# First query tile of chunk 0 finished first and copied out in fp32, last query tile in its bank, key banks and VectorE's order changed

## The chip, the cores and the metric

The kernel runs on one core of a Trainium2 chip. Its engines work in parallel, each through its own queue in order: TensorE (PE in the profile; its weight loads are PEld), VectorE (DVE), ScalarE (ACT), GpSimd (POOL), and SyncE (SP), whose queue issues the DMAs. They wait for each other through semaphores. The metric is the device time of one execution in microseconds; three runs of the kernel before gave 827.88, 828.29 and 828.38 us, a median of 828.29.

## The reference

One transformer layer over 2048 tokens of width 1024, in bf16. A conditioning vector `c` gives six rows of scales and shifts. A layer norm, scaled and shifted, feeds a linear attention of 32 heads; a second one feeds a gated feed-forward of width 3584; both are added back to `x`. What matters here is the front of the attention:

```python
mod = (_silu(c) @ w_mod).reshape(c.shape[0], 6, 1, -1)
sa, ca, ga, sb, cb, gb = (mod[:, 0].copy(), ..., mod[:, 5].copy())
h = _layernorm(x, axis=-1) * (1 + ca) + sa
...
phi = lambda t: jnp.where(t > 0, t + 1, jnp.exp(t)) + 1e-06
pq, pk = (phi(q), phi(k))          # q, k, v are the three thirds of h @ wqkv
kv = jnp.einsum('bhsd,bhse->bhde', pk, v)
z = jnp.einsum('bhsd->bhd', pk)
num = jnp.einsum('bhqd,bhde->bhqe', pq, kv)
den = jnp.einsum('bhqd,bhd->bhq', pq, z)[..., None] + 1e-06
```

## The kernel before

The program is recorded as one list of operations; each is put on its engine's queue in the order in which it is written. `auto` (line 168) records an operation, `add` (line 130) finds whom it must wait for: overlapping bytes in SBUF, and in PSUM whole banks (`self.excl`, line 156): an operation waits for the last access of every other engine to the same 2 KB bank. There is no scheduler: the written order is the order on each queue, and all operations carry the line of the recording helper, L176.

The 2048 tokens are handled in four chunks of 512, each of four x tiles of 128 tokens. The normalised tile is transposed by a DMA on SP's queue (`th_dma`, line 493) into `HT`, which has two buffers, and there scaled and shifted (`th_mod`, line 497; `MODCOL` holds the columns). For a chunk, a group of 8 products (128 weight columns by 512 tokens) gives one eighth of the queries (`q_group`, line 708) or keys (`k_group`, line 715) in one PSUM bank; `next_bank` (line 703) hands out the banks.

The function `phi` is made from a bank by `phi_evac` (line 665) and `phi_flush` (line 677). ScalarE writes an exponential to a slot of `E1` (four slots, in turn), and for queries also a relu to `RL`. When two groups have been through ScalarE, VectorE does the pair: a minimum with 1 on each slot, then for keys a pass that reads the bank once more and writes `PKT` (two buffers), for queries an addition into `PQT`. A key bank is thus free when VectorE has read it, a query bank when ScalarE has.

Chunk 0's queries are special (`q_phase_chunk0`, line 773), since the modulation columns are still being made from arriving weights. Seven of the eight query tiles, in banks 1, 2, 3, 4, 6, 7, 5, are accumulated in parts while the columns come (`q_part`, line 696). Bank 0 collects the columns of scale, shift and bias: `mod_sc` (line 508) makes shift columns out of `WSA`, `fin_sa` (line 519) copies them out, `bias_mm` (line 532) makes from them what the missing shift of the first four eighths of the inner dimension would have added to the queries, and `bias_fin` (line 538) copies it to `BIASQ`. The shift itself is put on these parts of `HT` afterwards (`h0_shift`, line 528), for the keys. The eighth query tile is computed in bank 0 after `bias_fin`. Then ScalarE makes exponential and relu of all eight tiles with `BIASQ` as bias (`q_phi`, line 759), into `E1` and `RL` for tiles 0 to 3, `E1X` and `RLX` for tiles 4 to 7; `q_min` and `q_add` (lines 763 and 768) are VectorE's part.

Around it stands the layer norm of chunk 1's x tiles 4 to 7: tile 4's sums by ScalarE (`act_stats`, line 578), the others' by VectorE (`ln_ops`), then a power on GpSimd (`ln1_rstd1`, `ln1_rstd2`, `pool_pow`), a normalising pass on VectorE and the transpose. Tile 5 goes first, then 4, 6 and 7.

After that come the eight key groups of chunk 0, with side work taken from `kside` (line 852) behind groups 1, 3 and 4: `th_mod` of chunk 1, each eighth in two halves of 256 tokens, the last query pair (6, 7), and ScalarE's sums for x tiles 10 and 11. Chunk 1 then begins with its own key groups (`chunk`, line 870), which read the whole 512 tokens of each eighth of `HT`.

Of the kernel before, what the change touches and what calls it, by code (L numbers as in the profile page):

```python
# [262 lines left out]
def bass_adaLN_cond__linear_attn_block__swiglu_ffn__prompt_kernel(  # L263
# [22 lines left out]
    with ExitStack() as es:  # L286
# [6 lines left out]
        def T(name, off, shape, dt):  # L293
            n = 1
            for s_ in shape[1:]:
                n *= s_
            assert off % 32 == 0 and off + n * mybir.dt.size(dt) <= ARENA, (name, off, shape)
            return nc.alloc_sbuf_tensor_at(name, shape, dt, offset=base + off)
# [49 lines left out]
        RLX = T("rlx", 196 * KB, [128, 4, 512], BF16)  # L348
        ACC = T("acc", 192 * KB, [128, D], FP32)
# [178 lines left out]
        def h0_shift(dt):  # L528
            P.dve("tensor_scalar", out=HT[:, 0, dt, :], in0=HT[:, 0, dt, :], scalar1=MODCOL[:, 1, dt:dt + 1],
                  scalar2=None, op0=ALU.add)  # L530
# [172 lines left out]
        def next_bank():  # L703
            i = qk_ctr[0]
            qk_ctr[0] += 1
            return (1, 2, 3, 4, 6, 7, 5, 0)[i % 8] if i < 40 else i % 5 + 1
# [48 lines left out]

        def q_slot(nt):
            return (E1, RL) if nt < 4 else (E1X, RLX)

        def q_phi(nt, bank):
            for buf, fn_ in zip(q_slot(nt), (ACT.Exp, ACT.Relu)):  # L760
                P.act("activation", out=buf[:, nt % 4, :], in_=PS[:, bank, :], func=fn_, bias=BIASQ[:, nt:nt + 1])

        def q_min(nts):
            for nt in nts:
                e = q_slot(nt)[0][:, nt % 4, :]
                P.dve("tensor_scalar", out=e, in0=e, scalar1=1.0, scalar2=1e-6, op0=ALU.min, op1=ALU.add)

        def q_add(nts):
            for nt in nts:
                e, r = q_slot(nt)  # L770
                P.dve("tensor_tensor", out=PQT[:, nt, 0:512], in0=r[:, nt % 4, :], in1=e[:, nt % 4, :], op=ALU.add)

        def q_phase_chunk0():
# [14 lines left out]
            act_stats(4, (0,))  # L788
# [15 lines left out]
            for nt in range(7):  # L804
                if nt == 1:
                    mod_sc(WSA, 0, range(4), range(4))
                if nt == 3:
                    mod_sc(WSA, 0, range(4), range(4, 8))
                    fin_sa(0, 4, True)
                    ln_ops[1][0]()  # L810
                if nt == 5:
                    bias_mm(range(4))
                    bias_fin()
                q_part(nt, qb[nt], (7,))
# [3 lines left out]
            for i, dt in enumerate((4, 5, 0, 1, 2, 3, 6, 7)):  # L818
                P.pe("matmul", out=PS[:, 0, :], lhsT=WQK[:, dt, 896:1024], rhs=HT[:, 0, dt, :], start=(i == 0),
                     stop=(i == 7))  # L820
            for dt in range(4):
                h0_shift(dt)
            ln1_xn(5)
            th_dma(5)
            for nt in range(2):
                q_phi(nt, qb[nt])
            act_stats(4, (1,))
            for nt in range(2, 8):
                q_phi(nt, qb[nt] if nt < 7 else 0)
# [9 lines left out]
            q_min((0, 1))  # L839
# [3 lines left out]
            q_add((0, 1))  # L843
            for nts in ((2, 3), (4, 5)):
                q_min(nts)
                q_add(nts)
# [8 lines left out]
        for c0 in (0, 256):  # L855
            for dt in range(NDT):
                add(kside, 1, lambda dt=dt, c0=c0: th_mod(1, dt, c0, c0 + 256))
        add(kside, 1, lambda: q_min((6, 7)))
        add(kside, 1, lambda: q_add((6, 7)))
        for jj, k in ((0, 3), (1, 4)):  # L860
            add(kside, k, lambda jj=jj: act_stats(10 + jj))
# [386 lines left out]
```

## Time and profile before

| what | us |
| --- | --- |
| median of the three runs | 828.29 |
| the profiled execution's own time | 827.71 |
| its span | 826.0 |
| TensorE busy with products | 816.3 |
| VectorE busy | 312.2 |
| ScalarE busy | 197.0 |
| GpSimd busy | 41.0 |

The granted clock of TensorE is 1.00. The span is the time from the first to the last instruction of the profiled execution; the execution's own time has a little around it. The views in order of time list, for one engine, start, length, the operation with the tile that it writes and those that it reads, and in brackets how long the engine had been idle and who ended that. Neighbours of one kind are merged into one row, whose length goes from the first start to the last end. The stage of the change lies between 24 and 60 us: chunk 0's queries end near 29 us, its keys near 43 us, and chunk 1's keys follow.

### The profile page before, as it was taken

To read this page: it belongs to the slowest core of one execution; us is meant where nothing else is said; L and a number is where in the kernel's file an instruction comes from. 1 tells how busy PE (TensorE), PEld (TensorE's weight loads), DVE (VectorE), ACT (ScalarE), POOL (GpSimd) and SP (SyncE) were. 2 spreads that over 40 slices of the span, in tenths; PEclk is the share of its full clock that TensorE was granted. 3 is DMA by queue.
4 is the path that set the end of the run, shared out by engine and by line. 5 is a ranking of instruction groups with operands and counts; after the bars stand their busy time and mean duration, and the time that the engine had idled before them with its cause. 6 is when DMAs were issued, how large, how long until landed. Compare 5 with 4: busy or idle time off the path is not lost.

```text
span 826.0 us, 10436 instructions
## 1 busy us (share of the span) xinstructions
PE 816.3 (99%) x4243; PEld 375.9 (46%) x4322; DVE 312.2 (38%) x672; ACT 197.0 (24%) x338; POOL 41.0 (5%) x58
## 2 busy tenths in 40 slices
PE   8999999999999999999999999999999999999998
PEld 4544444444444444444444444444444444444444
DVE  5798988477945521111221112122111111221111
ACT  4758642123341111011111101111110111111011
POOL 1110000000130000020000003000000300000000
DMA  9969756865698995600455570045557004553000
GB/s 316 297 139 223 167 159 149 181 175 211 149 253 245 296 249 153 166 26 26 136 151 151 153 174 25 23 131 153 151 152 182 27 19 126 151 152 88 0 26 26
DMA packets 199392, 119.32 MB, mean 144 GB/s; under 512 B 58024, under 2 KB 183088, under 8 KB 199344
## 3 DMA queue, kind: packets, MB, share of 16 engines
q1 hardware_dynamic: 199328, 118.65, 53.8%
q8 instruction: 34, 0.56, 0.3%
q14 instruction: 14, 0.11, 0.0%
q10 hardware_dynamic: 16, 0.00, 0.0%
HBM read 100.67 MB, written 4.33 MB: 127 GB/s over the span
## 4 chain that ended last, share of the span: by engine, by line
PE 98%; issue 1%; DMA 0%; DVE 0%; POOL 0%; SPq 0%
PE ps L176 98%; DMA xres<-in_A_x_dram 0%; POOL rstd L176 0%; DVE xres L176 0%; DVE stats L176 0%; SPq L176 0%; DVE ht L176 0%; DVE ve L176 0%; DVE mv L176 0%; DVE modcol L176 0%
## 5 line engine op out<-in xcount | busy, mean ns | idle before, releaser
L176 PE MATMUL ps<-h2t,gug 128*128 128x512 bf16 x878 | 210.1, 379 | 0.9
L176 PE MATMUL ps<-h2t,guu 128*128 128x512 bf16 x878 | 209.9, 379 | 0.9
L176 DVE TENSOR_TENSOR at<-sg,ps 128x512 bf16<-128x512 bf16 x112 | 77.0, 687 | 282.8 <-PE ps L176 270.6
L176 ACT ACTIVATE sg<-ps 128x512 bf16<-128x512 f32 x112 | 66.9, 597 | 309.7 <-PE ps L176 298.3
L176 PEld LDWEIGHTS ps<-h2t,guu 128*128 128x128 bf16 x896 | 87.7, 98 | 105.7
L176 PEld LDWEIGHTS ps<-h2t,gug 128*128 128x128 bf16 x896 | 87.6, 98 | 105.5
L176 PE MATMUL ps<-wd_a,at 128*128 128x512 bf16 (+1 forms) x502 | 111.9, 377 | 0.5
L176 PE MATMUL ps<-ht,wqk 128*128 128x512 bf16 x499 | 110.7, 379 | 0.9 <-DVE ht L176 0.2
L176 PE MATMUL ps<-wd_b,at 128*128 128x512 bf16 (+1 forms) x377 | 84.6, 377 | 0.4
L176 PEld LDWEIGHTS ps<-wd_a,at 128*128 128x128 bf16 x512 | 50.1, 98 | 59.6
L176 DVE TENSOR_TENSOR ut<-att,gb_b 128x512 bf16<-128x512 bf16 (+1 forms) x32 | 13.6, 426 | 167.5 <-ACT att L176 167.5
L176 PEld LDWEIGHTS ps<-ht,wqk 128*128 128x128 bf16 x512 | 49.2, 98 | 58.9 <-DVE ht L176 1.0
L176 ACT ACTIVATE att<-ps 128x512 bf16<-128x512 f32 (+1 forms) x32 | 17.4, 591 | 182.1 <-PE ps L176 182.1
L176 PEld LDWEIGHTS ps<-wd_b,at 128*128 128x128 bf16 x384 | 37.6, 98 | 44.7
L176 PE MATMUL ps<-pk,xres 128*128 128x512 bf16 x250 | 55.4, 379 | 0.6 <-issue 0.5
L176 PE MATMUL ps<-mw,pqt 128*128 128x512 bf16 x249 | 55.4, 379 | 0.5 <-issue 0.2
L176 POOL TENSOR_SCALAR h2t<-h2t,modcol 128x512 bf16<-128x512 bf16 x32 | 26.5, 846 | 383.0 <-DMA h2t<-xn 383.0
L176 ACT ACTIVATE e<-ps 128x512 bf16<-128x512 f32 x56 | 33.3, 611 | 31.8 <-PE ps L176 15.8
L176 ACT ACTIVATE junk<-xres 128x1024 bf16<-128x1024 bf16 x26 | 27.6, 1063 | 45.9 <-DVE xres L176 34.2
L176 PEld LDWEIGHTS ps<-mw,pqt 128*128 128x128 bf16 x256 | 24.8, 98 | 30.0 <-issue 0.5
L176 PEld LDWEIGHTS ps<-pk,xres 128*128 128x128 bf16 x256 | 24.6, 98 | 30.1 <-issue 1.3
L176 DVE SCALAR_TENSOR_TENSOR xres<-ps,xres 128x512 bf16<-128x512 f32 x32 | 21.5, 688 | 11.6 <-PE ps L176 11.3
(111 smaller groups left out, 337.8 us busy)
## 6 DMA issues: line engine op xcount, KB each, us to landing
gug<-in_B_w_gate_dram SPq DMA_DIRECT2D x56, 512.0 KB, 4.0
guu<-in_B_w_up_dram SPq DMA_DIRECT2D x56, 512.0 KB, 5.3
xres<-in_A_x_dram SPq DMA_DIRECT2D x20, 256.0 KB, 4.4
rb<-recip_den SPq DMA_DIRECT2D x8, 512.0 KB, 11.7
stgx<-in_w_mod_dram SPq DMA_DIRECT2D x2, 2048.0 KB, 9.3
wd_a<-in_B_w_down_dram SPq DMA_DIRECT2D x4, 1024.0 KB, 7.7
out_dram<-xres SPq DMA_DIRECT2D x31, 128.0 KB, 1.7
xres<-in_A_x_dram SPq DMA_DIRECT2D x3, 1024.0 KB, 6.5
```

Of the source, the lines that this page charges most:

```text
L176: return getattr(e, method)(**kw)
```

## The change

- Query tile 0 gets its last product first, and ScalarE copies its bank, without bias, to a new fp32 tile `QRAW`. Tile 0's exponential and relu are made from that copy, and come last of the eight (`QORD`). The four slots of `E1` and `RL` now hold tiles 1 to 4, those of `E1X` and `RLX` tiles 5, 6, 7 and 0.
- The eighth tile (tile 7) is computed in bank 1, which tile 0 has left. Its products stand around the last shift products, `fin_sa` and the bias products, in the order 0 to 7.
- Both passes of ScalarE's sums for x tile 4 come behind the copy; before, one stood earlier and one between the tiles' exponentials.
- On VectorE the four `h0_shift` come directly behind `bias_fin`, ahead of the rest of tile 5's statistics.
- The banks of chunk 0's key groups are 0, 2, 3, 4, 6, 7, 5, 1, and later groups up to the fortieth use 0, 2, 3, 1, 4, 6, 7, 5 in turn.
- Chunk 1's first halves of `th_mod` come ahead of the key groups, the second halves behind key group 1. The query pairs at positions 4 and 6 come behind key group 3. The sums of x tiles 10 and 11 come behind key groups 4 and 5 in place of 3 and 4.

```diff
@@ -346,6 +346,7 @@
         RL = T("rl", 188 * KB, [128, 4, 512], BF16)
         E1X = T("e1x", 192 * KB, [128, 4, 512], BF16)
         RLX = T("rlx", 196 * KB, [128, 4, 512], BF16)
+        QRAW = T("qraw", 202 * KB, [128, 512], FP32)
         ACC = T("acc", 192 * KB, [128, D], FP32)
         MHL = T("mhl", 196 * KB, [128, 2, D], BF16)
         MHLT = T("mhlt", 192 * KB, [128, 2 * NDT, 128], BF16)
@@ -703,7 +704,9 @@
         def next_bank():
             i = qk_ctr[0]
             qk_ctr[0] += 1
-            return (1, 2, 3, 4, 6, 7, 5, 0)[i % 8] if i < 40 else i % 5 + 1
+            if i < 8:
+                return (0, 2, 3, 4, 6, 7, 5, 1)[i]
+            return (0, 2, 3, 1, 4, 6, 7, 5)[i % 8] if i < 40 else i % 5 + 1
 
         def q_group(ch, nt):
             buf, bank = ch % 2, next_bank()
@@ -753,22 +756,30 @@
             P.wait_for("sp", [wr])
             P.dma("mdr%d" % i, dst[:], MDR[i].unsqueeze(0).to_broadcast([128, D]))
 
+        QORD = (1, 2, 3, 4, 5, 6, 7, 0)
+
         def q_slot(nt):
-            return (E1, RL) if nt < 4 else (E1X, RLX)
-
-        def q_phi(nt, bank):
+            i = QORD.index(nt)
+            bufs = (E1, RL) if i < 4 else (E1X, RLX)
+            return [t[:, i % 4, :] for t in bufs]
+
+        def q_phi(nt, src):
             for buf, fn_ in zip(q_slot(nt), (ACT.Exp, ACT.Relu)):
-                P.act("activation", out=buf[:, nt % 4, :], in_=PS[:, bank, :], func=fn_, bias=BIASQ[:, nt:nt + 1])
+                P.act("activation", out=buf, in_=src, func=fn_, bias=BIASQ[:, nt:nt + 1])
 
         def q_min(nts):
             for nt in nts:
-                e = q_slot(nt)[0][:, nt % 4, :]
+                e = q_slot(nt)[0]
                 P.dve("tensor_scalar", out=e, in0=e, scalar1=1.0, scalar2=1e-6, op0=ALU.min, op1=ALU.add)
 
         def q_add(nts):
             for nt in nts:
                 e, r = q_slot(nt)
-                P.dve("tensor_tensor", out=PQT[:, nt, 0:512], in0=r[:, nt % 4, :], in1=e[:, nt % 4, :], op=ALU.add)
+                P.dve("tensor_tensor", out=PQT[:, nt, 0:512], in0=r, in1=e, op=ALU.add)
+
+        def q_pair(i):
+            q_min(QORD[i:i + 2])
+            q_add(QORD[i:i + 2])
 
         def q_phase_chunk0():
             qb = [1, 2, 3, 4, 6, 7, 5]
@@ -785,7 +796,6 @@
                     for dt in (4, 5):
                         h0_scale_only(dt)
                 q_part(nt, qb[nt], (2, 3))
-            act_stats(4, (0,))
             for nt in range(7):
                 if nt == 6:
                     mod_sc(WSA, 0, range(6, 8))
@@ -802,31 +812,31 @@
                     bias_mm((4, 5))
                 q_part(nt, qb[nt], (6,))
             for nt in range(7):
-                if nt == 1:
+                q_part(nt, qb[nt], (7,))
+                if nt == 0:
+                    P.act("activation", out=QRAW[:], in_=PS[:, qb[0], :], func=ACT.Copy)
+                    act_stats(4)
+            for i, dt in enumerate(range(NDT)):
+                if i == 1:
                     mod_sc(WSA, 0, range(4), range(4))
-                if nt == 3:
+                if i == 3:
                     mod_sc(WSA, 0, range(4), range(4, 8))
                     fin_sa(0, 4, True)
                     ln_ops[1][0]()
-                if nt == 5:
+                if i == 5:
                     bias_mm(range(4))
                     bias_fin()
-                q_part(nt, qb[nt], (7,))
+                P.pe("matmul", out=PS[:, qb[0], :], lhsT=WQK[:, dt, 896:1024], rhs=HT[:, 0, dt, :], start=(i == 0),
+                     stop=(i == 7))
+            for dt in range(4):
+                h0_shift(dt)
             ln_ops[1][1]()
             ln_ops[1][2]()
             ln1_rstd1(5)
-            for i, dt in enumerate((4, 5, 0, 1, 2, 3, 6, 7)):
-                P.pe("matmul", out=PS[:, 0, :], lhsT=WQK[:, dt, 896:1024], rhs=HT[:, 0, dt, :], start=(i == 0),
-                     stop=(i == 7))
-            for dt in range(4):
-                h0_shift(dt)
             ln1_xn(5)
             th_dma(5)
-            for nt in range(2):
-                q_phi(nt, qb[nt])
-            act_stats(4, (1,))
-            for nt in range(2, 8):
-                q_phi(nt, qb[nt] if nt < 7 else 0)
+            for nt in QORD:
+                q_phi(nt, QRAW[:] if nt == 0 else PS[:, qb[nt % 7], :])
             for f in ln_ops[2]:
                 f()
             act_var(4)
@@ -836,14 +846,14 @@
             ln1_rstd2(6)
             ln1_xn_sum(4)
             th_dma(4)
-            q_min((0, 1))
+            q_min(QORD[0:2])
             for st in (6, 7):
                 ln1_xn(st)
                 th_dma(st)
-            q_add((0, 1))
-            for nts in ((2, 3), (4, 5)):
-                q_min(nts)
-                q_add(nts)
+            q_add(QORD[0:2])
+            q_pair(2)
+            for dt in range(NDT):
+                th_mod(1, dt, 0, 256)
             qk_ctr[0] = 0
 
         def add(d, k, f):
@@ -852,12 +862,11 @@
         kside = {}
         ln_ops = [ln1_stats_ops(4 + jj) for jj in range(4)]
 
-        for c0 in (0, 256):
-            for dt in range(NDT):
-                add(kside, 1, lambda dt=dt, c0=c0: th_mod(1, dt, c0, c0 + 256))
-        add(kside, 1, lambda: q_min((6, 7)))
-        add(kside, 1, lambda: q_add((6, 7)))
-        for jj, k in ((0, 3), (1, 4)):
+        for dt in range(NDT):
+            add(kside, 1, lambda dt=dt: th_mod(1, dt, 256, 512))
+        for i in (4, 6):
+            add(kside, 3, lambda i=i: q_pair(i))
+        for jj, k in ((0, 4), (1, 5)):
             add(kside, k, lambda jj=jj: act_stats(10 + jj))
         q_phase_chunk0()
         for st in range(12, 16):
```

## The prediction

> **What bounds the kernel now.** I read the page's busy shares and chain first, then the weight loads of TensorE in order of time, which show the stage of the change, then VectorE and ScalarE there.
>
> ```profile
> PE 816.3 (99%) x4243; PEld 375.9 (46%) x4322; DVE 312.2 (38%) x672; ACT 197.0 (24%) x338; POOL 41.0 (5%) x58
> PE 98%; issue 1%; DMA 0%; DVE 0%; POOL 0%; SPq 0%
> ```
>
> TensorE is the chain, so a microsecond in which it stands still is a microsecond of the result, unless a later stop shrinks by as much. Its pitch is 0.2158 us for a 512-column product: the chain in order of time has pieces that start at 30.82 and 41.61, 50 products apart. So a group of 8 takes 1.73 us. I number the key groups of chunk 0 as groups 0 to 7 and go on with chunk 1 (8, 9, ...). Weight loads after 42 us:
>
> ```profile
> 43.39 0.10 PEld L176 LDWEIGHTS ps<-ht,wqk 128*128 128x128 bf16 x1 [0.16 <-DVE ht L176]
> 44.66 1.62 PEld L176 LDWEIGHTS ps<-ht,wqk 128*128 128x128 bf16 x9 [0.16 <-DVE ht L176]
> 46.75 3.14 PEld L176 LDWEIGHTS ps<-ht,wqk 128*128 128x128 bf16 x16 [0.46 <-DVE pkt L176]
> ```
>
> These are the only stops there. Group 8 follows the second halves of `ht` at their pace (43.39, 43.64 and so on to 44.66: six steps of 0.256, 0.24 us lost). Group 10, at 46.75, waits for VectorE to read group 2 out of its bank: 0.56 between two loads, 0.34 lost. So 0.58 us is all that a better order can win here. Nothing is lost at the eighth query tile: the products around the bias columns stay on pitch. Group 11 loads at 46.75 + 8 x 0.2158 = 48.48.
>
> VectorE is the full engine of this stage (its column is the third pair; windows of 4 us):
>
> ```profile
> 36.00:40.00 4.00, 4.00 (x20) 1.85 (x19) 3.75 (x14) 4.00 (x9) 0.00 (x0) 1.00 1.37 174
> 40.00:44.00 4.00, 3.95 (x20) 1.75 (x18) 4.00 (x16) 3.94 (x8) 0.00 (x0) 1.00 1.02 323
> ```
>
> Its order of work, with start and length:
>
> ```profile
> 27.33 0.17 DVE L176 COPY biasq<-ps 128x8 f32<-128x8 f32 x1 [0.38 <-PE ps L176]
> 27.41 0.68 DVE L176 BATCH_NORM_STATS2 stats<-xres 128x6 f32<-128x512 bf16 x1
> 28.37 0.15 DVE L176 TENSOR_SCALAR ve<-mv 128x1 f32<-128x1 f32 x1
> 28.44 1.13 DVE L176 TENSOR_SCALAR ht<-ht,modcol 128x512 bf16<-128x512 bf16 x4
> 29.49 0.54 DVE L176 TENSOR_SCALAR xres<-xres,mv,rstd 128x1024 bf16<-128x1024 bf16 x1
> 30.15 1.29 DVE L176 BATCH_NORM_STATS2 stats<-xres 128x6 f32<-128x512 bf16 x2
> ...
> 33.50 0.54 DVE L176 TENSOR_SCALAR xres<-xres,sumx,rstd 128x1024 bf16<-128x1024 bf16 x1
> 33.96 0.49 DVE L176 TENSOR_SCALAR e<-e 128x512 bf16<-128x512 bf16 x2
> ...
> 37.30 0.49 DVE L176 TENSOR_SCALAR e1x<-e1x 128x512 bf16<-128x512 bf16 x2
> ...
> 40.43 4.18 DVE L176 TENSOR_SCALAR ht<-ht,modcol 128x256 bf16<-128x256 bf16 x16
> 44.53 0.48 DVE L176 TENSOR_SCALAR e1x<-e1x 128x512 bf16<-128x512 bf16 x2
> ...
> 45.61 0.48 DVE L176 TENSOR_SCALAR e<-e 128x512 bf16<-128x512 bf16 x2
> ...
> 47.23 0.48 DVE L176 TENSOR_SCALAR e<-e 128x512 bf16<-128x512 bf16 x2
> ...
> 50.48 1.28 DVE L176 BATCH_NORM_STATS2 stats<-xres 128x6 f32<-128x512 bf16 x2
> ```
>
> What to see: the `ht` halves end at 44.5, a query pair takes 1.08 (44.53 to 45.61), an evacuated key pair 1.62 (45.61 to 47.23), and group 7 leaves its bank only at 50.48.
>
> **The change part by part.**
>
> *TensorE's products, the fp32 copy.* The products are the same in number. Those of the eighth tile move into bank 1, which must first be copied out. Tile 0's last product starts at 24.40; the copy (about 0.69, the reads of `ps` on ScalarE nearby) begins when that product ends, at 24.8, and is done by 25.6. Six products of the other tiles cover it until 25.9. One copy of 0.7 us is added to an idle ScalarE: it waits 11.5 us before 25.55 for an x tile. Cost 0; if the cover failed, under 0.7.
>
> *Bias columns later.* Seven products (two last ones of tiles 5 and 6, five of the eighth) now stand ahead of the bias products: 7 x 0.2158 = 1.51. `biasq` moves from 27.33 to 28.84. Bank 0 is now awaited by group 0, three products behind the bias products, 0.65 us, where the answer took 0.42 (27.13 to 27.55): no stop. ScalarE's first exponential moves from 27.59 to 29.1; both statistics passes over x tile 4 fit before it (25.55 plus 2 x 1.15). Its 16 passes at 0.57 end at 38.25 instead of 37.77. Group 1 needs the first bank at 31.0 and gets it at 30.4: covered.
>
> *VectorE's queue.* After `biasq` come the four shifts (28.92 to 29.97), then statistics to `ve` (27.41 to 28.37, 0.96 long): `ve` at 30.93. In the order before, the shifts stood behind `ve` and hid GpSimd's power:
>
> ```profile
> 28.61 0.74 POOL L176 TENSOR_TENSOR rstd<-ve,neghalf 128x1 f32<-128x1 f32 x1 [18.37 <-DVE ve L176]
> ```
>
> Now the normalising pass of tile 5 follows `ve` directly and waits 0.24 + 0.74 with nothing in between: 31.95, against 29.49, 2.46 later. 0.20 is regained, as 29.49 to 30.15 is 0.66 where this pass takes 0.46 (33.50 to 33.96). So 2.26 later from there, and two query pairs end at 37.30 + 2.26 = 39.56.
>
> *First halves of `ht`, moved ahead.* They need the transposes of tiles 5 and 4. SP's queue gets both later: tile 4's was issued at 34.07, now at 33.50 + 0.54 + 2.26 = 36.3. The seven `ht` transposes from 24 to 60 us, and that tile's own 4.2:
>
> ```profile
> DMA to landing us min/median/max: 3.2/4.2/7.3
> ```
>
> I take 4.2, its own row: landing 40.5. Lowest 3.2 gives 39.5 (no wait); highest 7.3, from a transpose behind a queue of x loads, gives 43.6. So the halves run 40.5 to 42.6 (8 x 0.261, from 4.18 for 16); pair 0,1 to 44.2 (1.62); the second halves to 46.3. Their transposes (tiles 6 and 7, by then issued by 39.9) land about 44.1: covered, by 0.1. Group 8 therefore ends about 46.5, group 9 loads at 46.6 and group 10 at 48.3, against 46.75: 1.6 lost. Group 10's bank is ready at 46.3 + 0.4 + 0.68 = 47.4, so its old stop of 0.34 goes.
>
> *The bank order.* It is now 0,2,3,4,6,7,5,1 for groups 0 to 7, then 0,2,3,1,4,6,7,5. Group 11, formerly in bank 4 behind group 3, now takes bank 1, which holds group 7: the last of the chunk to be evacuated. Behind the second halves VectorE has pair 2,3 (1.62), both delayed query pairs (2.16), pair 4,5 and pair 6,7 (47.23 to 50.48, 3.25): 46.3 + 7.03 = 53.35. ScalarE's last exponential for them comes near 50.4, in time. With 0.1 to the weight load, group 11 starts at 53.45 instead of 48.48. Before it, TensorE stands from 50.2 for 3.2 us. Even with VectorE exactly as before, group 11 would wait for 50.48.
>
> *After it.* Groups 12 to 15 take banks long free. VectorE lost 2.9 and TensorE 5.0, so it gains distance, and the next 80 us show no stop that could shrink. The distances at the change to five banks (groups 40 and 44) fall to five groups, which chunk 3 already lives with. Names alone change after that. ScalarE, SP and GpSimd do nothing that ends later than this.
>
> **Sum.** 53.45 - 48.48 = 4.97 us. On the profiled execution (span 826.0, time 827.71) that is 832.7; it ran 0.58 under the median of the runs, 828.29, from which it is 833.2.
>
> *A rule against it.* The opening shows TensorE slow when it has been idle:
>
> ```profile
> 2.61 4.47 PE L176 MATMUL ps<-e,ident 128*128 128x512 bf16 x13 [0.21 <-DVE e L176]
> ```
>
> Thirteen products span 4.09 from first start to last, against 12 x 0.2158 = 2.59: 1.5 us lost. No idle time after that is long enough in this trace to show a return. The Trainium skill (TensorE: Matmul & The Clock Gate, What's actually happening) says that an idle window of about 3.4 us brings back half rate; by that rule my stop of 3.2 stays just under, and a longer one would add the loss of the opening.
>
> **The rivals.**
> - *The slow opening returns* after the stop before group 11: 4.97 + 1.5, 834.7. For it: the stop is near what might do it. Against: group 8 to 10's products lie just before it.
> - *Transposes land late*, as the slowest row (7.3): the first halves start at 43.6, 3.1 later, all behind them too: 836.3. Against: the x loads in front of that row have mostly landed by 36.
> - *VectorE loses nothing*, only the bank waits, for 50.48: 50.6 - 48.48 = 2.1, less nothing: 830.4. For it: VectorE had some waits that could shrink. Against: `biasq` itself is 1.51 late.
> - *Faster: group 11's bank is free in time.* Then the early halves save the 0.58 and the time is 827.7. It decides at group 7's evacuation: before 48.4. Against: that ended at 50.48 in a queue without holes, and no VectorE instruction is taken out; 2 us of work would have to vanish.
>
> **How the numbers follow.** Chances: forecast 0.77, slow opening 0.08, late transposes 0.05, VectorE unmoved 0.07, faster 0.03. The forecast's own range is 832.2 (landing 3.2: 0.94 less) to 833.9 (landing 4.7, the second halves then late too). For 8 in 10 I reach down half way to the unmoved case and up to the slow opening: 831.5 to 834.9. About 0.2% (1.7 us) is what a measurement can tell from no change. Slower by more: all but the faster case and a little of the unmoved one, 0.94; within: 0.03; faster: 0.03.
>
> **What the profile after would show.** `biasq` near 28.8; the tile 5 pass near 31.9 behind GpSimd's `rstd`; a transpose ending the idle time before the first halves of `ht`, near 40.5; weight loads of group 8 spaced by 0.26 up to about 46.4; and one long stop of 3 us or more before group 11, ended by a `pkt` evacuation near 53. I am wrong if that stop is absent, or ends long before 52, or if products behind it are spaced by more than 0.22.

## The result, and the profile after

The changed kernel takes 833.46 us (median of 6, 832.52 to 837.27) against 828.12 us for the kernel before (median of 6 in the same sitting, 827.74 to 828.38): a ratio of 1.0071, 95% interval 1.0051 to 1.0091. It is slower, by 5.3 us. The profiled execution took 832.52 us with a span of 830.8 (before: 827.71 and 826.0), so in the profiles it is 4.8 us.

Three of the six executions show a mean granted TensorE clock of 1.000 and took 832.5 to 832.9, three show 0.996 to 0.998 and took 834.0 to 837.3, and the profile below is one at 1.000.

The busy shares and the chain of the changed kernel's page:

```profile
PE 821.5 (99%) x4322; PEld 376.3 (45%) x4322; DVE 313.4 (38%) x672; ACT 197.6 (24%) x339; POOL 40.6 (5%) x58
PE 96%; DVE 2%; DMA 1%; issue 0%; POOL 0%; DVEq 0%
```

TensorE was 98% of the chain and is 96% now; VectorE and DMAs have come into it. Where, the chain in order of time tells (start, length, what ran):

```profile
31.42 0.56 POOL rstd L176
31.98 0.03 issue
32.01 0.55 DVE xres L176
32.55 1.21 DVE stats L176 x2
...
35.99 0.40 POOL rstd L176
36.38 4.00 DMA ht<-xres
...
40.48 2.14 DVE ht L176 x8
42.62 0.41 DVE e L176 x2
...
44.25 2.06 DVE ht L176 x8
...
47.93 0.41 DVE e1x L176 x2
...
52.11 1.23 DVE pkt L176 x4
53.34 0.05 issue
53.39 775.20 PE ps L176 x3944
```

Read from the bottom: everything from 53.39 on is TensorE without a stop. It was let go by the evacuation of group 7 (52.11); that stood behind query pairs, the second halves of `ht`, the key pair 0,1 and the first halves in VectorE's queue; the first halves (40.48) waited for tile 4's transpose, issued at 36.38. That one waited for VectorE's normalising pass of tile 4, which ends at 36.35. (The chain names GpSimd's power of 35.99, which is that of tiles 6 and 7 and ended at the same time.) The pass of tile 4 stands in VectorE's queue behind the statistics of tiles 6 and 7 and the pass of tile 5, and this one waited for GpSimd (31.42).

The products of TensorE between 24 and 112 us, those rows that have idle time ahead of them (in brackets):

```profile
44.56 5.64 PE L176 MATMUL ps<-ht,wqk 128*128 128x512 bf16 x24 [1.03 <-DVE ht L176]
53.39 58.88 PE L176 MATMUL ps<-ht,wqk 128*128 128x512 bf16 x272 [3.18 <-DVE pkt L176]
```

Two stops, no others up to 112 us: 1.03 before group 8, which waits for the second halves, and 3.18 before group 11, which waits for bank 1. In between, group 8 follows the halves at 0.256 a product where the pitch is 0.216. The same view of the kernel before has no stop at all in these 88 us, though its weight loads halted at 43.39 to 46.75. Its last row, from 27.15 to the end of the window, has no bracket:

```profile
27.15 85.17 PE L176 MATMUL ps<-ht,wqk 128*128 128x512 bf16 x385
```

A bracket counts from the end that the profile gives a product, 0.38 behind its start, while the next one normally starts after 0.216. So a stop costs 0.16 more than its bracket: 1.19 and 3.34, and with 7 steps of 0.04 that is 4.8 us.

Group 12 loads at 54.91 instead of 50.01, 4.90 later. Of that, 0.25 is older, since the first part products of this execution already start at 23.57 where those of before do at 23.32. What remains, 4.65, is the 4.8 less 0.2 that before loses between its own products.

VectorE in order of time:

```profile
29.09 0.17 DVE L176 COPY biasq<-ps 128x8 f32<-128x8 f32 x1 [0.45 <-PE ps L176]
31.19 0.15 DVE L176 TENSOR_SCALAR ve<-mv 128x1 f32<-128x1 f32 x1
32.01 0.55 DVE L176 TENSOR_SCALAR xres<-xres,mv,rstd 128x1024 bf16<-128x1024 bf16 x1 [0.66 <-POOL rstd L176]
...
40.48 2.14 DVE L176 TENSOR_SCALAR ht<-ht,modcol 128x256 bf16<-128x256 bf16 x8 [0.79 <-DMA ht<-xres]
44.16 2.14 DVE L176 TENSOR_SCALAR ht<-ht,modcol 128x256 bf16<-128x256 bf16 x8
...
53.23 1.30 DVE L176 BATCH_NORM_STATS2 stats<-xres 128x6 f32<-128x512 bf16 x2
```

Every mark of the forecast is there: `biasq` 29.09 (28.84 was forecast, and the opening is 0.25 late), tile 5's pass at 32.01 behind `rstd` (31.95), the first halves at 40.48 behind a transpose (40.5), group 7 out of its bank at 53.23 (53.35), the stop before group 11 3.18 (3.2).

That the marks are met says that the sum is right. It does not say that each link is a price: a link is one only if the time falls when it is taken out. That is what the experiments ask.

### The profile page after: what moved, and what is told of

It is laid out like the page before. It is cut to its first block, busy times and chain, and to the rows that moved or that the text cites. A ratio compares the mean times of both kernels' runs of the same rounds, so it can differ in the third digit from the quotient of the medians.

```text
span 830.8 us, 10516 instructions
## 1 busy us (share of the span) xinstructions
PE 821.5 (99%) x4322; PEld 376.3 (45%) x4322; DVE 313.4 (38%) x672; ACT 197.6 (24%) x339; POOL 40.6 (5%) x58
## 4 chain that ended last, share of the span: by engine, by line
PE 96%; DVE 2%; DMA 1%; issue 0%; POOL 0%; DVEq 0%
PE ps L176 96%; DVE ht L176 1%; DVE pkt L176 1%; DMA ht<-xres 0%; DVE stats L176 0%; DMA cs<-in_c_dram 0%; DVE e L176 0%; DVE pqt L176 0%; POOL rstd L176 0%; DVE xres L176 0%; DVE e1x L176 0%; DVE mv L176 0%; DVE ve L176 0%; DVE biasq L176 0%; DVEq L247 0%
## 5 line engine op out<-in xcount | busy, mean ns | idle before, releaser
L176 PE MATMUL ps<-ht,wqk 128*128 128x512 bf16 x512 | 112.5, 379 | 4.2 <-DVE pkt L176 3.2
L176 PEld LDWEIGHTS ps<-wd_b,at 128*128 128x128 bf16 x384 | 37.6, 98 | 44.7
```

What stands on the lines that cost most here:

```text
L176: return getattr(e, method)(**kw)
```

## The experiments

Times are medians in us; each ratio is to the kernel before, run in the same sitting (828.37, 827.93 and 827.80 in the three sittings). A throwaway product or pass, where there is one, adds work whose result nobody uses.

| run | median | ratio, 95% interval | stops of TensorE in the profiled run (us) |
|---|---|---|---|
| changed kernel again | 834.46 | 1.0071 (1.0058 to 1.0083) | 1.40 group 8, 3.18 group 11, then 7 products at half rate |
| bank order alone | 830.39 | 1.0030 (1.0018 to 1.0042) | 1.96 group 11 |
| change, straight order | 832.16 | 1.0048 (1.0034 to 1.0061) | 1.51 group 8, 0.48 group 24, 1.24 group 40 |
| change, straight order to group 31 | 830.61 | 1.0034 (1.0023 to 1.0045) | 1.50 group 8, 0.49 group 24 |
| change, query pairs behind the key pairs | 831.56 | 1.0043 (1.0029 to 1.0056) | 1.76 group 8, 1.55 group 11 |
| change, shifts behind the statistics | 834.89 | 1.0086 (1.0073 to 1.0100) | 0.86 group 8, 3.18 group 11, then 14 products at half rate |
| change, bias columns early | 833.03 | 1.0067 (1.0051 to 1.0082) | 1.05 group 8, 3.19 group 11 |
| change, stop filled with products | 833.19 | 1.0062 (1.0049 to 1.0074) | 1.25 group 8, 0.37 group 11 |
| change, longer stop | 839.10 | 1.0134 (1.0120 to 1.0148) | 1.66 group 8, 6.99 group 11, then 14 products at half rate |
| change, three of its parts mended | 830.83 | 1.0036 (1.0023 to 1.0050) | 0.68 group 8, 0.26 group 18, 0.58 group 24 |
| change, three undone | 829.74 | 1.0024 (1.0014 to 1.0034) | 0.92 group 8, 0.50 group 24 |
| early halves alone | 828.59 | 1.0004 (0.9995 to 1.0013) | none |

### What does the bank order cost?

The first run gives the kernel before the changed bank order from group 8 on, with bank 0 in the place of bank 1, so that group 11 again follows group 7; nothing else moves.

```diff
-            return (1, 2, 3, 4, 6, 7, 5, 0)[i % 8] if i < 40 else i % 5 + 1
+            if i < 8:
+                return (1, 2, 3, 4, 6, 7, 5, 0)[i]
+            return (1, 2, 3, 0, 4, 6, 7, 5)[i % 8] if i < 40 else i % 5 + 1
```

> The kernel before, with one thing of the change: from group 8 on the bank of the last key group of chunk 0 comes fourth (1, 2, 3, 0, 4, 6, 7, 5). Theory (the fourth bank waits for group 7's evacuation): group 11 cannot load before 50.5 us where it loaded at 48.5, so one stop of about 2 us appears, ended by pkt, and the time is 2.0 us over before, about 830.1. Rival (the order of the banks does not matter, VectorE's later queue is the whole cause): no stop at group 11, the time of before, 828.1.

830.39, 2.0 us more than before. The products of TensorE, with idle time:

```profile
51.00 61.25 PE L176 MATMUL ps<-ht,wqk 128*128 128x512 bf16 x277 [1.96 <-DVE pkt L176]
```

One stop of 1.96 before group 11, ended by VectorE's evacuation, and the time is longer by just that. The mechanism is shown by itself, and its bare price is 2.0 us with VectorE's queue untouched.

The other way round, the changed kernel with the straight order (group i + 8 on the bank of group i):

```diff
-            return (0, 2, 3, 1, 4, 6, 7, 5)[i % 8] if i < 40 else i % 5 + 1
+            return (0, 2, 3, 4, 6, 7, 5, 1)[i % 8] if i < 40 else i % 5 + 1
```

> The changed kernel with the bank order put back to one round of eight (0, 2, 3, 4, 6, 7, 5, 1 throughout). Theory: group 11 then follows group 3, free at 47.8, and loads at about 50.0 without a stop; groups 12 to 15 just find their banks free; what is left is the 1.5 us stop at group 8, so 3.3 us of the loss goes: about 829.3 to 829.8, 1.2 to 1.6 over before. Rival (VectorE's delay sets the time whatever the bank): the stop moves to a later group and the time stays over 832.

832.16: hardly any gain, where much was expected. The products:

```profile
44.91 29.16 PE L176 MATMUL ps<-ht,wqk 128*128 128x512 bf16 x131 [1.51 <-DVE ht L176]
74.56 26.99 PE L176 MATMUL ps<-ht,wqk 128*128 128x512 bf16 x120 [0.48 <-ACT ht L176]
102.78 9.45 PE L176 MATMUL ps<-ht,wqk 128*128 128x512 bf16 x43 [1.24 <-ACT rl L176]
```

The stop before group 11 is gone, and two others have come. The one at 102.78 is made by the edit: group 39 gets bank 1, and so does group 40, the first of the five-bank part. (The changed order has bank 1 as its fourth, which keeps them five groups apart.) The one at 74.56, inside group 24 (the first of chunk 2), is not: there TensorE waits for ScalarE's share of the next `ht`. The changed kernel, with its longer stop before group 11, shows no such wait. So the edit was mended, with bank 1 in the middle of the last eight:

```diff
-            return (0, 2, 3, 1, 4, 6, 7, 5)[i % 8] if i < 40 else i % 5 + 1
+            if i < 32:
+                return (0, 2, 3, 4, 6, 7, 5, 1)[i % 8]
+            return (0, 2, 3, 4, 1, 6, 7, 5)[i % 8] if i < 40 else i % 5 + 1
```

> The changed kernel with one straight round of banks (0, 2, 3, 4, 6, 7, 5, 1) up to group 31 and 0, 2, 3, 4, 1, 6, 7, 5 for groups 32 to 39, so that bank 1 is not used by groups 39 and 40 one behind the other, as it was in the other trial of the straight order. Theory: the stop of 1.6 us at group 40 goes and nothing else changes: stops of 1.6 at group 8 and together 1.2 in groups 25 to 26, which wait for ht from ScalarE; about 830.4, 2.0 to 2.6 over before. Rival (the straight round costs as much elsewhere): 832 again.

830.61, and the products show what is left:

```profile
44.91 29.16 PE L176 MATMUL ps<-ht,wqk 128*128 128x512 bf16 x133 [1.50 <-DVE ht L176]
74.56 37.78 PE L176 MATMUL ps<-ht,wqk 128*128 128x512 bf16 x173 [0.49 <-ACT ht L176]
```

The changed kernel's executions at a clock of 1.000 took 832.3 to 832.9, so the order is worth about 2.0 us inside the change as well, although the stop that it makes there is 3.18. By the starts of the products, 0.9 of the difference is the late work of ScalarE, which comes out in group 24 as soon as it is not hidden under the longer stop: 0.65 at the stop and 0.26 two products on. The other 0.5 is the stop at group 8, 1.50 here and 1.03 in the changed kernel's profile, because tile 4's transpose landed at 40.7 and not at 40.4. The other 2.7 us of loss have another source.

### What do VectorE's order and the opening cost?

Three edits of the changed kernel each take out one link of the chain above, and a fourth takes out several at once. First, the two delayed query pairs go behind the key pairs:

```diff
-            add(kside, 3, lambda i=i: q_pair(i))
+            add(kside, 7, lambda i=i: q_pair(i))
```

> The changed kernel with its two delayed query pairs moved from behind key group 3 to behind key group 7 in VectorE's queue, bank order as changed. Theory: VectorE reaches group 7's evacuation 2.0 to 2.16 us earlier, group 11 loads at about 51.3 in place of 53.4, and the time falls by as much, to about 830.6 to 831. Rival (the pairs were hidden work): nothing moves, over 832.4.

831.56. The products before groups 8 and 11, and VectorE's first halves:

```profile
45.21 5.64 PE L176 MATMUL ps<-ht,wqk 128*128 128x512 bf16 x24 [1.76 <-DVE ht L176]
52.40 59.96 PE L176 MATMUL ps<-ht,wqk 128*128 128x512 bf16 x271 [1.55 <-DVE pkt L176]
```

```profile
41.13 2.14 DVE L176 TENSOR_SCALAR ht<-ht,modcol 128x256 bf16<-128x256 bf16 x8 [1.31 <-DMA ht<-xres]
```

The stop before group 11 fell from 3.18 to 1.55, by 1.63, less than the 2.16 of the two pairs: after them ScalarE's last exponential is what group 7 waits for. Of that, 0.65 went again, because in this execution tile 4's transpose landed later (first halves at 41.13, not 40.48). The queue position of two query pairs is a real price of about 1 us net.

Second, the statistics of tile 5 go ahead of the four shifts, so that the shifts cover GpSimd's power again, as they did before:

```diff
-            for dt in range(4):
-                h0_shift(dt)
             ln_ops[1][1]()
             ln_ops[1][2]()
             ln1_rstd1(5)
+            for dt in range(4):
+                h0_shift(dt)
             ln1_xn(5)
```

> The changed kernel with the four shifts put back behind ve on VectorE, so that they cover GpSimd's power again. Theory: the wait of 0.66 us ahead of tile 5's pass goes, everything behind it on VectorE and on SP comes 0.7 earlier, group 11 loads near 52.7 and the time is 0.6 to 0.8 lower in executions at clock 1.000, about 831.8. Rival (the transposes land as late as before, whatever VectorE does): no change, 832.5.

834.38 to 835.67, no gain. VectorE's first halves:

```profile
40.70 2.14 DVE L176 TENSOR_SCALAR ht<-ht,modcol 128x256 bf16<-128x256 bf16 x8 [1.49 <-DMA ht<-xres]
```

They start at 40.70, not earlier than in the changed kernel; VectorE has done the rest sooner and stands 1.49 instead of 0.79. Tile 4's transpose was issued 0.5 earlier (35.89) and landed 0.2 later. All four executions have a clock below 1, so the median can't be set against 832.5 to 832.9; the stop before group 11, 3.18 in both, can.

Third, the shift and bias products go back between the last products of the seven tiles, where they stood before, and all else stays changed:

```diff
             for nt in range(7):
+                if nt == 1:
+                    mod_sc(WSA, 0, range(4), range(4))
...
+                if nt == 5:
+                    bias_mm(range(4))
+                    bias_fin()
                 q_part(nt, qb[nt], (7,))
...
             for i, dt in enumerate(range(NDT)):
-                if i == 1:
-                    mod_sc(WSA, 0, range(4), range(4))
...
```

> The changed kernel with only the shift and bias products put back among the last products of the first seven tiles, ahead of the eighth tile; bank order and VectorE's order as changed. Theory: biasq comes 1.5 us earlier, VectorE's whole queue with it, as far as the transposes allow; group 11 loads near 52.0 in place of 53.4, and the time is 1.2 to 1.5 lower, about 831.2. Rival (the later columns were covered): no change, 832.5.

833.03 (832.38 to 833.42 at a clock of 1.000): no gain either. The products before group 11 and VectorE's waits:

```profile
53.30 58.88 PE L176 MATMUL ps<-ht,wqk 128*128 128x512 bf16 x266 [3.19 <-DVE pkt L176]
```

```profile
DVE ht L176 <- DMA ht<-xres: 1.7, 1, 1.7
```

The time won at the bias columns is lost again, all of it (tile 4's transpose issued at 35.35, landed at 40.3), in the wait for the transpose: first halves at 40.40, a stop of 3.19.

So neither link of the opening is a price by itself: the transpose of tile 4 lands at 40 to 41 us whichever is taken out. The fourth run takes out three at once, the bank order as mended, the query pairs behind the key pairs, and the shifts behind the statistics:

```diff
+            return (0, 2, 3, 4, 1, 6, 7, 5)[i % 8] if i < 40 else i % 5 + 1
...
             ln1_rstd1(5)
+            for dt in range(4):
+                h0_shift(dt)
...
+            add(kside, 7, lambda i=i: q_pair(i))
```

> The changed kernel with three things put right at once: the straight bank order (as mended), the delayed query pairs behind key group 7, the shifts behind ve. The bias columns stay 1.5 us late. Theory (VectorE's late start is a cause of its own): a stop of 1 to 1.5 us at group 8 stays, and some of the stop at groups 25 and 26: 829.2 to 830. Rival (bank, pairs and power are the whole cause): 828.0, as before.

830.83, no better than the straight order to group 31 by itself (830.61). First halves at 40.09, behind a wait of 1.31; the products:

```profile
44.17 17.72 PE L176 MATMUL ps<-ht,wqk 128*128 128x512 bf16 x79 [0.68 <-DVE ht L176]
62.16 11.61 PE L176 MATMUL ps<-ht,wqk 128*128 128x512 bf16 x52 [0.26 <-DVE pkt L176]
74.35 38.00 PE L176 MATMUL ps<-ht,wqk 128*128 128x512 bf16 x170 [0.58 <-ACT ht L176]
```

The stop before group 8 is 0.8 shorter than with the straight order by itself, and the most of that comes back as waits at groups 18 and 24. The query pairs stand behind the second halves in VectorE's queue, so they have no part in the stop before group 8.

Next, bank order, statistics and bias columns all undone; the first query tile, its fp32 copy, the eighth tile in bank 1, and the order of halves and pairs stay changed:

```diff
+            return (0, 2, 3, 4, 1, 6, 7, 5)[i % 8] if i < 40 else i % 5 + 1
...
+                if nt == 5:
+                    bias_mm(range(4))
+                    bias_fin()
                 q_part(nt, qb[nt], (7,))
...
             ln1_rstd1(5)
+            for dt in range(4):
+                h0_shift(dt)
```

> The changed kernel with the straight bank order (as mended), the shifts behind ve, and the shift and bias products back among the last products of the first seven tiles, ahead of the eighth tile; kept are the tile finished first, its fp32 copy, the eighth tile in bank 1, the halves and the query pairs as changed. Theory (these three terms are the whole loss): biasq near 27.4, no stop at groups 8, 11 or 25, and the time of before, 827.6 to 828.3. Rival (copy, tile order or pairs cost as well): 829 or more.

829.74, still 1.9 us over before. VectorE's first halves and the products:

```profile
40.69 2.14 DVE L176 TENSOR_SCALAR ht<-ht,modcol 128x256 bf16<-128x256 bf16 x8 [2.47 <-DMA ht<-xres]
```

```profile
44.77 29.16 PE L176 MATMUL ps<-ht,wqk 128*128 128x512 bf16 x131 [0.92 <-DVE ht L176]
74.43 37.78 PE L176 MATMUL ps<-ht,wqk 128*128 128x512 bf16 x169 [0.50 <-ACT ht L176]
```

Tile 4's transpose is issued at 34.90 now, 1.48 earlier than in the changed kernel, and lands 0.2 later. VectorE stands in front of the first halves for 2.47 us with the finished key pair 0,1 behind them in its queue; all that follows is late, up to ScalarE's `ht` in group 24.

Last, the kernel before with only the order of halves and pairs: first halves behind three query pairs and ahead of key pair 0,1, second halves behind it, pair 6,7 behind the key pair 2,3.

```diff
+            for dt in range(NDT):
+                th_mod(1, dt, 0, 256)
...
-        for c0 in (0, 256):
-            for dt in range(NDT):
-                add(kside, 1, lambda dt=dt, c0=c0: th_mod(1, dt, c0, c0 + 256))
-        add(kside, 1, lambda: q_min((6, 7)))
-        add(kside, 1, lambda: q_add((6, 7)))
+        for dt in range(NDT):
+            add(kside, 1, lambda dt=dt: th_mod(1, dt, 256, 512))
+        add(kside, 3, lambda: q_min((6, 7)))
+        add(kside, 3, lambda: q_add((6, 7)))
```

> The kernel before, with only the order of the halves on VectorE changed: the first halves of ht ahead of the key pair 0,1, the second halves behind it, the last query pair behind key pair 2,3; query tiles, banks and the rest as before. Theory: without the 1.5 us later bias columns this order is good: the second halves end near 44.2, so group 8 no longer follows them at 0.256 a step and group 10's bank is free in time; the 0.58 us of stops go: about 827.5. Rival (the order of the halves itself costs): group 8 waits for halves that come later, 829 or more.

828.59, the same as before. VectorE's first halves, which wait for nothing:

```profile
38.66 2.14 DVE L176 TENSOR_SCALAR ht<-ht,modcol 128x256 bf16<-128x256 bf16 x8
```

Here the transpose was issued at 34.36 and landed at 37.8, and three query pairs cover it. No stop is left from group 8 on, and yet nothing is won. Groups 8 to 15 take 13.81 us by their weight loads, where before took 14.00: 0.19 is all that the stops of before cost, not 0.58, and 0.19 of 828 is below what these runs can tell.

All the landings of tile 4's transpose side by side, issue and landing in us from the rows of each profiled run:

```
kernel before                 34.07  38.3      longer stop                   36.03  40.7
early halves alone            34.36  37.8      straight order to group 31    36.26  40.7
bank order alone              34.70  38.9      changed kernel                36.38  40.4
three undone                  34.90  40.6      straight order                36.47  40.7
bias columns early            35.35  40.3      query pairs behind key pairs  36.50  41.0
three parts mended            35.46  40.0      stop filled                   36.70  40.9
shifts behind the statistics  35.89  40.6      changed kernel again          36.95  41.3
```

Issued by 34.70 it landed by 38.9. Issued from 34.90 to 36.38 it landed at 40.0 to 40.7, and not in the order of issue. The last four, at 36.47 to 36.95, landed at 40.7 to 41.3. So there is a step, and behind it a delay of the issue by 1.5 us moved the landing by nothing that can be told: two profiles of the unaltered changed kernel, 0.57 apart in the issue, lie 0.9 apart in the landing. What makes the step is open. Tile 5's transpose (landing at 36.7 to 40.0) is in flight beside it in all of these runs, and a load of x tile 11 (35.8 to 37.6) in all but the first profile of the changed kernel; no run isolates either.

### Why do executions differ?

The unaltered changed kernel again, for a profile of an execution below 1.000:

> The changed kernel once more, unaltered, as the yardstick for the two that follow. Of its six executions so far three showed a mean granted clock of 0.996 to 0.998 and times of 834.0 to 837.3, three showed 1.000 and 832.5 to 832.9; the kernel before shows 1.000 in all 23. Theory (the stop of 3.2 us at group 11 sometimes brings TensorE's slow state back): again a part of the executions, a third to two thirds, below 1.000 and 1.5 us or more longer. Rival (chance of that chip): all at 1.000.

832.31 and 832.69 at a mean granted clock of 1.000; 834.46, 834.91 and 835.02 at 0.998. The profile is of one of the latter. Its windows around the stop (from:to, length, products' busy time, granted clock, DMA share, GB/s):

```profile
50.00:53.00 3.00, 1.15 (x6) 1.00 1.07 178
53.00:54.30 1.30, 0.00 (x0) 0.82 0.00 0
54.30:57.30 3.00, 2.96 (x8) 0.51 0.68 128
57.30:60.00 2.70, 2.70 (x14) 1.00 0.28 52
```

Up to the stop the clock is 1.00. Within it, it starts to fall, is 0.51 for three microseconds behind it, and then full again. In these three microseconds 7 products start about 0.427 apart, twice the pitch: 7 x 0.21 = 1.5 us lost, as much as at the opening. The clock records put the half rate at 53.85 to 57.26, which is 3.41 us. In the two other profiles that show it, it lasts twice that (shifts behind the statistics, 52.72 to 59.54) and three times (longer stop, 53.24 to 63.47). In all three it begins 2.3 to 2.8 us behind the end of the last product, so while TensorE still stands. If the stop is the cause, products that fill it must end it, and a longer stop must bring it every time. For the filler, 13 throwaway products into a bank that is free there, between groups 10 and 11:

```diff
+                if ch == 1 and gi == 3:
+                    for _ in range(13):
+                        P.pe("matmul", out=PS[:, 4, :], lhsT=WQK[:, 0, 0:128], rhs=HT[:, 1, 0, :], start=True, stop=True)
```

> The changed kernel with 13 more products of 512 columns between groups 10 and 11, into bank 4, which group 12 overwrites: work that is thrown away and fills 2.8 us of the stop. Theory of the slow state: TensorE is never idle long enough, so all executions show a clock of 1.000, none is over 833.5, median 832.7. Rival (the low clock has another cause, or more products cost time): the share of low clocks is as without them, or the median is 2.8 us higher.

The stop, in the products of TensorE, is short now. Group 11 starts at 53.93, 0.54 later than in the changed kernel's profile, as does group 8 already (45.11 against 44.56):

```profile
53.93 58.45 PE L176 MATMUL ps<-ht,wqk 128*128 128x512 bf16 x270 [0.37 <-DVE pkt L176]
```

832.77 to 833.42, five of five at a clock of 1.000. For the longer stop, 12 throwaway passes on VectorE ahead of group 7's evacuation:

```diff
+        for _ in range(12):
+            add(kside, 5, lambda: P.dve("tensor_scalar", out=E1X[:, 0, :], in0=RLX[:, 0, :], scalar1=1.0, scalar2=1e-6,
+                                        op0=ALU.min, op1=ALU.add))
```

> The changed kernel with 12 more VectorE passes of 0.20 us over a finished slot, whose result is thrown away, ahead of group 7's evacuation: the stop at group 11 is 2.4 us longer, 5.6 us. Theory (group 7's evacuation alone sets group 11, and a longer stop brings the slow state in nearly every execution): group 11 loads at about 55.8; the time is 2.4 over the changed kernel in executions at clock 1.000, and most executions are below 1.000 with another 1.5 us or more, median about 836.5. Rival (no slow state): 834.9 to 835.2 in all of them.

```profile
57.47 54.70 PE L176 MATMUL ps<-ht,wqk 128*128 128x512 bf16 x239 [6.99 <-DVE pkt L176]
```

This line, again from TensorE's products, shows 6.99 of idle time, 3.81 more than 3.18: the twelve passes took 3.90 us and not the 2.4 that was reckoned. All four executions are below 1.000 (0.994 to 0.996), 838.41 to 839.81; behind the stop 14 products go at half rate, 3.0 us lost. Group 11 starts at 57.47, 4.1 behind the changed kernel's 53.39; 832.5 + 4.1 + 3.0 = 839.6, and the profiled execution took 839.81.

Over all runs, by the longest stop of the profiled one: up to 1.3 us, no execution below 1.000 (28 of the filled kernel, the three parts mended, the three undone and the early halves, and all of before); 1.5 to 2.0, 2 of 21 (one with the bank order alone, one with the straight order to group 31); 3.2, 11 of 19 (the changed kernel 6 of 11, shifts behind the statistics 4 of 4, bias columns early 1 of 4); 7.0, 4 of 4. A stop of TensorE makes the slow clock return, and the longer it is the more often. How long the stop was in the executions without a profile, the two with 1.5 to 2.0 among them, is not known. In the three profiles that show it the loss is 7 or 14 products at half rate.

## Why the prediction was right, and where not

**The time, the sign and the bank: right.** 833.2 was forecast (828.29 + 4.97 is 833.26) and 833.46 measured. That the two are so close is in part luck. No execution took 833.46: it is the middle between three at a clock of 1.000 and three below. The sum knew only the first kind, whose median, 832.60, is 4.5 over before and not 4.97. The step on the bank order said that group 11 would wait for group 7's evacuation, start at 53.45 and stand 3.2; it started at 53.39 after 3.18. The order put alone on the kernel before makes the same stop, at the place that the step gave for VectorE as it was, and with the price (2.1 said; 1.96 of idle time and 2.0 in the median found).

**The fp32 copy and the reordered products: right, at nothing.** The copy ran from 25.06 to 25.66 in the changed kernel's profile, and TensorE has no stop there. The kernel with three parts undone keeps both, and its TensorE has no stop between 24 us and group 8 either.

**"Only 0.58 us to win": mis-sized, 0.2.** The term was read off gaps between weight loads. The products are what counts, and they lost 0.2. Early halves alone take every one of these stops away and win nothing that can be measured. The baseline of the sum, group 11 at 48.48, came off the same gaps and was right by accident: in before the weights of group 11 load at 48.28, but its first product starts at 48.49. The change's own loss in the profile is 4.90 - 0.25 = 4.65. The forecast of 4.97 is 0.3 over that, and 4.90 looks nearer because the opening of that execution ran 0.25 late. The Trainium skill (TensorE: Matmul & The Clock Gate, Architectural detail) says that TensorE can pull weight loads ahead of products still in flight; the trace agrees: in before, each load starts while the product ahead of its own still runs, and where two loads are 0.56 apart (46.19 and 46.75) the products are 0.35 apart, 0.13 over the pitch.

**Bias columns 1.51 later, tile 5's pass 2.46 later: the times were right, but each alone was no price.** The prediction let the first halves follow the issue of the transpose at a fixed 4.2 us, so that each delay of the issue went into the sum. With the bias columns back (issue 1.03 earlier) or the statistics back (0.49 earlier), the halves started at 40.40 and 40.70, against 40.48, and the time did not fall. The step that failed is "landing 40.5 = 36.3 + 4.2" as a sum: issued anywhere from 34.90 to 36.38 the transpose landed at 40.0 to 40.7, so 4.2 was only what made the two meet, and that 40.5 was met to 0.1 is luck. What costs, by the traces, is the next step, the first halves put ahead of key pair 0,1 in an in-order queue: as soon as the transpose is not there, VectorE stands with finished work behind it. With the bank order and the opening put back 1.9 us are left, and the products of that run lose them where `ht` is late, at group 8 and in group 24. With three query pairs ahead of the halves and a transpose at 37.8 the order costs nothing. No run puts the old order of the halves into the changed kernel, so the 1.9 are read from a trace and not from taking this link out.

**"Nothing later shrinks": right only with the long stop in place.** In the changed kernel TensorE has no stop after group 11. Without the 3.18 before group 11 the late work of ScalarE comes out in group 24, 0.9 us in all. This, and a stop at group 8 that was 0.5 longer in that profile, is why undoing the bank order returns 2.0 us and not 3.2. Taken out one after the other, the parts are 2.0 for the bank order (to 830.61), 0.7 for the opening (to 829.74; the intervals of these two ratios overlap, so it is hardly told from nothing) and 1.9 for the halves ahead of a late transpose.

**The rivals.** "The slow opening returns" was given 0.08, at 834.7. It happened in 6 of 11 executions of the unaltered kernel, at 834.0 to 835.0 and once 837.3, so it is no rival but a second outcome of the same kernel, and the median of 833.46 lies between the two. The mechanism was right, and the size (1.5) for the five up to 835.0; what the one at 837.3 lost no profile shows. The chance was wrong. By the Trainium skill (TensorE: Matmul & The Clock Gate, What's actually happening) the window is about 3.4 us long and free-running. Taken as a threshold on the stop, which is how the prediction took it, that keeps 3.2 safe, and the runs contradict it: with stops of 3.2 the clock fell in 11 executions of 19. That the window is free-running would make the return a matter of chance, which the runs bear out; that stops of 1.5 to 2.0 should do it at all (2 in 21) the figure of 3.4 doesn't explain.

"VectorE loses nothing" and "faster" are refuted by the chain: the stop was ended at 53.3, not at 50.48 or before 48.4. "Transposes land late" didn't happen at its price of 7.3, but its mechanism, the first halves waiting for a transpose with all else behind them, is the one that the experiments left standing. It was hidden in the forecast's own 4.2.

No version beat the kernel before. The nearest, early halves alone, equals it.

## What to carry to other kernels

When a kernel's PSUM banks are handed on in a new order, set beside each new user the time at which the old one is evacuated: a bank whose holder is last in VectorE's queue must go to the last taker. Don't put work that needs a DMA ahead of finished evacuations in an in-order queue, unless the landing, not only the issue, is well before its turn. Size a stop by the starts of the products, not by the weight loads, and count on a surcharge behind a long stop of TensorE: here 1.5 to 3 us in the profiles that show it, in 11 of 19 executions with a stop of 3.2 and in 2 of 21 with 1.5 to 2.0.

## What the runs showed of the hardware that was not expected

- TensorE's mean clock was below 1.000 in 11 of 19 executions with stops of 3.2 us, and in 2 of 21 where the longest stop was 1.5 to 2.0. Three profiles show how: half rate (0.427 us a product) for 3.41 us or two or three times that, beginning 2.3 to 2.8 us into the stop. Behind 3.2 us it cost 7 products in one profile and 14 in another, 1.5 and 3.0 us of loss. With thirteen products of filler none of five executions showed it.
- A transpose of 128x1024 bf16 from SBUF landed 3.4 to 5.7 us after its issue, and the landing did not follow the issue evenly: 34.07 to 34.70 gave 37.8 to 38.9, 34.90 gave 40.6, and 36.38 gave 40.4. Why is open.
- A pass of VectorE over 128x512 bf16 into the same slot, twelve times in a row, took 3.90 us for all, one every 0.33, where a pair of passes in place on two slots takes 0.50 from the start of the first to the end of the second, with 0.29 for one pass. Which difference between the two makes it was not tested.
